# The last 34 rows of w_down: three small loads into 46 partitions, or seven, four of which bring two rows each into one partition

## The chip, the cores and the metric

The kernel runs on one core of one Trainium2 chip. The metric is the device time of one execution in microseconds (us). The kernel before takes 376.3 us, the median of 3 runs (376.07 to 376.39). PE is TensorE, DVE is VectorE, ACT is ScalarE, POOL is GpSimd, SP is SyncE, whose only work here is to issue DMAs.

## The reference, cut to what matters

One decode step for two batch rows, all float32: a layer norm, attention of 32 heads over the last 2048 keys and values of the cache, a bilinear GLU beside it, and the sum of both with x.

```python
xn = _layernorm(x)                                  # x: 2 x 1 x 512
q = xn @ wq                                         # 32 heads of 128
p = softmax(q . k_cache[:, :, -2048:] * 128**-0.5)
A = (p . v_cache[:, :, -2048:]) @ wo                # 4096 x 512
h = (xn @ w_gate) * (xn @ w_up)                     # 1376 wide
B = h @ w_down                                      # w_down: 1376 x 512
out = x + A + B
```

Nearly all bytes are keys, values and weights, each read once: some 159 MB.

## The kernel before, in words

**The stream.** The host lays keys, values and nearly all weights out in one array, `stream`, in the order of use. `blocks()` (lines 89 to 114) lists the loads, and `pump()` (182 to 203) issues them on SP's queue: first a small tile `first` (x and constants), then big `step` loads of up to 128 x 15872 floats (7936 KB) into three rotating buffers. A buffer is free when the last field in it has been used; `done()` (205 to 212) counts that, and calls `pump()`, which issues the next load into it. So the first three step loads are issued at the start, and the fourth waits for the buffer of the first (keys of heads 0 to 2), which DVE leaves after its third sum.

**The heads.** For each head DVE multiplies the keys by q (`products`) and sums along 128 elements (`sums`), 4.4 us each; POOL, ACT and DVE make the softmax; PE weighs the values and projects with `wo`, three heads behind.

**The GLU.** `project_gu` makes gate and up from the second step load, `gate()` (444 to 466) multiplies them and turns the 1376 values h into columns, with matmuls that each take a piece of h and an ACT copy out of PSUM each. `down`, `down_rest` (490 to 498) and `down_half` multiply by w_down. 1376 rows are 10 chunks of 128 and 96 more; of these 62 lie with x in the field `wr` of the stream.

**The tail.** The last 34 rows lie in an input of their own, `tail`, and come into the tile `wd_tail`, one row of 2 KB to a partition: 20 rows in partitions 0 to 19, 12 in 32 to 43, 2 in 44 and 45. `TG` and `TR` (46, 47) say so: runs of `OWN` = 4 rows, with an unused row in the input after each run, so that a load isn't one straight piece. Three loads on SP's queue (219 to 222) bring them, issued right behind the first three step loads. POOL clears the tile first (171). `gate()` makes the fitting columns of h in two pieces (462 to 466), and `down_rest` uses all 46 partitions in one product of two columns by 512 (497). `PADS` (49) are unused tiles that place the others in memory.

**Semaphores.** Each DMA signals its landing on one of eight semaphores, named DMAHW0 to DMAHW7, which the framework deals out in turn in the order of issue. A DMA that gets a semaphore that an earlier one had waits, on the issuing queue, until that earlier one has landed. All DMAs here but the first store are issued on SP, which works through its waits and issues strictly in order.

Of the kernel before, what the change touches and what calls it, by code (L numbers as in the profile page):

```python
# [8 lines left out]
F32 = mybir.dt.float32  # L9
# [7 lines left out]
P = 128  # L17
B, D, H, DH, SK, F = 2, 512, 32, 128, 8192, 1376
# [4 lines left out]
NFB = -(-F // FB)  # L23
# [5 lines left out]
M = B  # L29
# [12 lines left out]
RX = HP  # L42
FX = RX - M
FT = FR - FX
OWN = 4
TG = [(0, 5), (32, 3), (32 + 3 * OWN, 1)]
TR = [OWN, OWN, FT - 8 * OWN]
TP = TG[-1][0] + TR[-1]
PADS = 480, 376


def k(h):
# [36 lines left out]
def blocks():  # L89

    def wd(n):
        return [("wd", i, D) for i in range(*WD[n])]

    def gu(half):
        n = NC * (FH[half][1] - FH[half][0])
        return [("wg", half, n), ("wu", half, n)]

    ones = [("pick", 0, 8 * B), ("rows", 0, NFB * B)]
    first = [("x", 0, B * NC)] + ones + [("w", 0, NC * DH)]
    loads = [[("w", 1, CQ - NC * DH)] + k(0) + k(1) + k(2), gu(0) + k(3) + gu(1)]  # L100
    loads += [v(0) + wd(0) + [("wr", 0, HD)] + k(LAG + 1) + v(1)]
    order = [(h - (h >= EARLY), k, h) for h in range(LAG + 2, H - 1)]
    order += [(h + 0.5, v, h - LAG) for h in range(LAG + 2, H - 1)]
    order.sort(key=lambda n: n[0])
    loads += packed([f for _, fields, h in order for f in fields(h)])
    loads += [k(H - 1) + v(H - 1 - LAG) + wd(1)]
    out = [(("f", 0), first)] + [(("s", i), fields) for i, fields in enumerate(loads)]
    late, last = ("s", len(loads)), ("s", len(loads) + 1)
    out += [(late, v(H - 3) + [("vh", 0, CK // B)]), (late, v(H - 2)[:1])]
    out += [(last, [("vh", 1, CK // B)])]  # L110
    out += [(last, v(H - 2)[1:] + [("wo", H - 1, CO)] + wd(2))]
    halves = [("wh", (c, n), HD) for n in range(2) for c in range(WD[-1][1], NFC)]
    out += [(last, wd(3) + halves[:2])]
    return out + [(last, halves[i : i + 1]) for i in range(2, len(halves))]
# [33 lines left out]
def kernel(  # L148
# [8 lines left out]
    nc = tc.nc  # L157
    pe, dve, act, sp = (InOrder(tc, e) for e in (nc.tensor, nc.vector, nc.scalar, nc.sync))
# [3 lines left out]
    const = ctx.enter_context(tc.tile_pool(name="const", bufs=1))  # L162
# [4 lines left out]


    const.tile([P, PADS[0]], F32, name="pad0")
    wd_tail = const.tile([TP, D], F32, name="wd_tail")  # L170
    nc.gpsimd.memset(wd_tail, 0.0)

    todo, at = [], 0
    for key, fields in blocks():
# [30 lines left out]
    def done(kind, i):  # L205
        nonlocal held
        _, key = got.pop((kind, i))
        left[key] -= 1
        if left[key] == 0 and key[0] != "f":
            del tiles[key]  # L210
            held -= 1
            pump()
# [3 lines left out]
    pick = got["pick", 0][0].rearrange("p (r s b) -> p r s b", s=2, b=B)  # L216
    rows = got["rows", 0][0]

    g0 = 0
    for (r0, n), m in zip(TG, TR):  # L220
        sp.dma_start(wd_tail[r0 : r0 + n * m, :], tail[g0 : g0 + n, :m, :])
        g0 += n
    carry = rows[:M, :M]

    mean_w = const.tile([P, P], F32, name="mean_w")
# [6 lines left out]
    acc, acc_g = acc_t[:M, :], acc_t[:, :P]  # L232
# [15 lines left out]
    tr = ps_c.tile([P, 4 * P], F32, name="tr")  # L248
# [175 lines left out]

    hT = const.tile([P, 4, NFB, M], F32, name="hT")

    hX = const.tile([P, 3, M], F32, name="hX")
    dve.memset(hX, 0.0)

    def project_gu(half):  # L430
# [13 lines left out]
    def gate():  # L444
        g_sb = small.tile([P, FB], F32, name="o_sb", bufs=2)
        act.copy(g_sb, gu_ps[0])
        h_sb = small.tile([P, FB], F32, name="o_sb", bufs=2)
        dve.tensor_tensor(h_sb, g_sb, gu_ps[1], op=ALU.mult)
        for i in range(4):
            t = tr[:, P + i * P // 2 : P + i * P // 2 + NFB * B]  # L450
            pe.matmul(t, h_sb[:, i * P : (i + 1) * P], rows, start=True, stop=True)
            act.copy(hT[:, i, :, :], t.rearrange("p (n b) -> p n b", b=B))
        f = (NFC % 4) * P
        own = slice((NFB - 1) * B, NFB * B)
        for i in range(2):
            t = tr[HP * i : HP * i + RX, P + P // 4 : P + P // 4 + NFB * B]
            pe.matmul(t, h_sb[:, f - M : f + FX], rows, start=True, stop=True)
            act.copy(hX[HP * i : HP * i + RX, i, :], t[:, own])
            one = rows[HP * i : HP * i + M, 2 * i * B : 2 * i * B + B]
            act.copy(hX[HP * i : HP * i + M, i, :], one)  # L460
        f += FX
        for r0, r1 in ((0, TG[0][1] * OWN), (TG[1][0], TP)):
            t = tr[r0:r1, P + 3 * P // 4 : P + 3 * P // 4 + NFB * B]
            pe.matmul(t, h_sb[:, f : f + r1 - r0], rows, start=True, stop=True)
            act.copy(hX[r0:r1, 2, :], t[:, own])
            f += r1 - r0

    def down(n):
        for c in range(*WD[n]):
            if n < 2:  # L470
                pe.matmul(
                    acc, hT[:, c % 4, c // 4, :], got["wd", c][0],
                    start=False, stop=(c == WD[1][1] - 1),
                )
            else:
                accumulate(hT[:, c % 4, c // 4, :], got["wd", c][0])
            done("wd", c)
# [12 lines left out]
    def down_rest():  # L490
        wr = got["wr", 0][0]
        for i in range(2):
            pe.matmul(
                acc[:, HD * i : HD * i + HD], hX[: HP + RX, i, :], wr[: HP + RX],
                start=False, stop=False,
            )
        pe.matmul(acc, hX[:TP, 2, :], wd_tail, start=False, stop=False)
        done("wr", 0)


# [28 lines left out]
    for h in (H - 4, H - 3):  # L529
        products(h)  # L530
        if h == H - 3:
            for i, n in enumerate((FB, FB, FB, 448)):
                pe.matmul(
                    spare[:, :n], mean_w, got["k", h][0][:, i * FB : i * FB + n],
                    start=True, stop=True,
# [54 lines left out]
    down(3)  # L590
    const.tile([P, PADS[1]], F32, name="pad1")
    acc_late = spare[:, :HP]
# [18 lines left out]
def laid_out(x):  # L611

    import numpy as np

    a = x["A_x"].reshape(B, D)
    first = {
        kind: np.zeros((P, w), a.dtype) for kind, _, w in blocks()[0][1][:3]
    }
    first["x"][:] = a.reshape(B, P, NC).transpose(1, 0, 2).reshape(P, B * NC)
    for b in range(B):  # L620
        for r in range(4):
            for s in range(2):
                first["pick"][8 * s + 4 * b + r :: 32, (2 * r + s) * B + b] = 1.0
        for n in range(NFB):
            first["rows"][32 * n + b, n * B + b] = 1.0
    cache = {
        kind: x[name][:, :, SK - W :, :].reshape(B, H, P, J * DH).transpose(1, 2, 0, 3)
        for kind, name in (("k", "A_k_cache"), ("v", "A_v_cache"))
    }
    wq = x["A_wq"].reshape(P, NC, H // HG, GC).transpose(2, 0, 1, 3)  # L630
    wo = x["A_wo"].reshape(H, P, D)
    gu = {
        kind: x[name].reshape(P, NC, F)
        for kind, name in (("wg", "B_w_gate"), ("wu", "B_w_up"))
    }
    wd = x["B_w_down"]
    rest = wd[NFC * P :]
    mixed = np.zeros((2, HP, HD), a.dtype)
    mixed[:] = np.concatenate([a, rest[:FX]]).reshape(RX, 2, HD).swapaxes(0, 1)

    def field(kind, i):
        if kind in first:
            return first[kind]
        if kind == "k":
            return cache[kind][i].reshape(P, CK)
        if kind == "v":
            h, p0, p1 = i
            return cache[kind][h].reshape(P, CK)[:, p0 * FB : p1 * FB]
        if kind == "w":
            return (wq[0][:, :, DH:] if i else wq[0][:, :, :DH]).reshape(P, -1)  # L650
        if kind == "wq":
            return wq[i // HG + 1][:, i % HG, :]
        if kind == "wo":
            return wo[i]
        if kind == "wr":
            return mixed.reshape(P, HD)
        if kind == "vh":
            return cache["v"][H - 1][:, i]
        if kind == "wh":
            c, n = i  # L660
            return wd[c * P : (c + 1) * P].reshape(P, 4, 2, HP)[:, :, n].reshape(P, HD)
        if kind == "wd":
            return wd[i * P : (i + 1) * P]
        return gu[kind][:, :, FH[i][0] : FH[i][1]].reshape(P, -1)

    parts = [
        np.concatenate([field(kind, i) for kind, i, _ in fields], axis=1).ravel()
        for _, fields in blocks()
    ]
    groups_of = np.zeros((sum(n for _, n in TG), OWN + 1, D), a.dtype)  # L670
    r = FX
    for g in range(len(groups_of)):
        m = OWN if g < 8 else TR[-1]
        groups_of[g, :m] = rest[r : r + m]
        r += m
    return {
        "tail": groups_of,
        "stream": np.concatenate(parts),
    }

# [35 lines left out]
```

## Time and profile before

| | |
|---|---|
| time, median of 3 runs | 376.3 us |
| time of the profiled execution | 376.45 us |
| its span, first to last instruction | 374.7 us |
| read from HBM | 159.47 MB |
| mean of the DMA engines over the span | 426 GB/s |
| busy: PE, DVE, ACT, POOL | 69%, 79%, 15%, 7% |
| mean granted TensorE clock | 0.827 |

The span leaves out 1.75 us of the execution's time, before its first and after its last instruction. In the profile's rows the line is L132 for all that goes through the recording helper, so that rows are told apart by tiles: `out<-in`. A row of a timeline begins with start and duration in us, and ends with the engine's idle time ahead of it and what ended that. "DMA to landing" is from the start of the issuing instruction to the last of its data. A DMA share is the mean over 16 DMA engines; in windows of a few us it can go over 1, since a packet is counted where it begins.

### The profile page before, as it was taken

To read this page: it belongs to the slowest core of one execution; us is meant where nothing else is said; L and a number is where in the kernel's file an instruction comes from. 1 tells how busy PE (TensorE), PEld (TensorE's weight loads), DVE (VectorE), ACT (ScalarE), POOL (GpSimd) and SP (SyncE) were. 2 spreads that over 40 slices of the span, in tenths; PEclk is the share of its full clock that TensorE was granted. 3 is DMA by queue.
4 is the path that set the end of the run, shared out by engine and by line. 5 is a ranking of instruction groups with operands and counts; after the bars stand their busy time and mean duration, and the time that the engine had idled before them with its cause. 6 is when DMAs were issued, how large, how long until landed. Compare 5 with 4: busy or idle time off the path is not lost.

```text
span 374.7 us, 2900 instructions
## 1 busy us (share of the span) xinstructions
PE 259.6 (69%) x1108; PEld 89.9 (24%) x1108; DVE 294.7 (79%) x145; ACT 57.3 (15%) x260; POOL 25.7 (7%) x75
## 2 busy tenths in 40 slices
PE   3166696884597882685968705896565855599897
PEld 3132123231222221122312202222111211133244
DVE  3069999369979569999369999894599999999760
ACT  1002011110202210020112002112010210112131
POOL 1000000000001000000100000010000000000010
PEclk9999697799576886597788975889666899689999
DMA  8999999999999999999999999999999999999996
GB/s 344 420 438 467 466 408 441 434 434 428 429 428 434 434 434 434 429 434 434 434 429 428 434 434 434 434 429 435 434 434 434 435 427 434 434 434 420 422 419 266
DMA packets 4232, 159.70 MB, mean 426 GB/s; under 512 B 730, under 2 KB 986, under 8 KB 1276
## 3 DMA queue, kind: packets, MB, share of 16 engines
q1 hardware_dynamic: 4076, 159.50, 98.7%
q8 instruction: 8, 0.13, 0.1%
q10 hardware_dynamic: 144, 0.03, 0.0%
q14 instruction: 4, 0.03, 0.0%
HBM read 159.47 MB, written 0.07 MB: 426 GB/s over the span
## 4 chain that ended last, share of the span: by engine, by line
DMA 66%; PE 18%; DVE 14%; ACT 1%; issue 1%; SPq 0%; DVEq 0%
DMA step<-in_stream_dram 66%; DVE s L132 7%; DVE step L132 7%; PE q L132 6%; PE o_ps L132 6%; PE acc L132 4%; PE tr L132 2%; ACT o_sb L132 1%; ACT oT L132 0%; DVE m L132 0%; DVE o_out L132 0%; SPq L132 0%; DVE rec L132 0%; DVEq L132 0%
## 5 line engine op out<-in xcount | busy, mean ns | idle before, releaser
L132 DVE TENSOR_TENSOR step<-step,q 128x4096 f32<-128x4096 f32 x31 | 136.8, 4412 | 45.2 <-DMA step<-in_stream_dram 41.1
L132 DVE TENSOR_REDUCE s<-step 128x32 f32<-128x4096 f32 x32 | 141.4, 4419 | 1.1
L132 PE MATMUL o_ps<-step,p 128*16 128x512 f32 x512 | 76.1, 659 | 45.3 <-DMA step<-in_stream_dram 45.3
L132 PE MATMUL q<-step,xnb 128*128 128x512 f32 (+1 forms) x128 | 76.1, 742 | 31.9 <-DMA step<-in_stream_dram 31.9
L132 PEld LDWEIGHTS q<-step,xnb 128*128 128x128 f32 x128 | 29.2, 244 | 84.1 <-issue 67.1
L132 PE MATMUL acc<-step,oT 128*2 128x512 f32 (+1 forms) x88 | 39.6, 612 | 8.5 <-ACT oT L132 8.5
L132 PE MATMUL tr<-first,o_sb 128*128 128x2 f32 (+4 forms) x192 | 29.9, 274 | 15.8 <-ACT o_sb L132 11.9
L132 PEld LDWEIGHTS o_ps<-step,p 128*16 128x16 f32 x512 | 13.7, 100 | 98.0 <-DMA step<-in_stream_dram 54.7
L132 PEld LDWEIGHTS tr<-first,o_sb 128*128 128x128 f32 (+2 forms) x192 | 27.2, 216 | 39.8 <-ACT o_sb L132 33.7
L132 ACT COPY o_sb<-o_ps 128x512 f32<-128x512 f32 x23 | 13.5, 586 | 145.7 <-PE o_ps L132 145.6
L331 POOL PARTITION_ALL_REDUCE mm<-m x32 | 11.5, 358 | 240.2 <-DVE rec L132 135.4
L132 ACT ACTIVATE nm<-mm 128x2 f32<-128x2 f32 x32 | 6.6, 206 | 128.6 <-POOL mm L331 128.6
L347 POOL PARTITION_ALL_REDUCE sum<-rs x32 | 12.8, 400 | 97.7 <-ACT p L132 97.7
L132 ACT ACTIVATE p<-s,nm 128x16 f32<-128x16 f32 x64 | 19.2, 300 | 1.0
L132 PE MATMUL o_ps<-step,xn 128*2 128x512 f32 (+1 forms) x48 | 14.9, 683 | 5.9 <-DMA step<-in_stream_dram 5.9
L132 ACT ACTIVATE oT<-tr,rec 128x1 f32<-128x1 f32 x64 | 12.1, 260 | 27.9 <-PE tr L132 27.9
L132 DVE TENSOR_TENSOR step<-step,tr 128x4096 f32<-128x4096 f32 x1 | 4.4, 4422 | 15.2 <-DMA step<-in_stream_dram 15.2
L132 ACT ACTIVATION_READ_ACCUMULATOR p<-s,nm 128x1 f32 x64 | 12.0, 187 | 0.0
L132 PE MATMUL q<-xnb,mean_w 128*128 128x512 f32 (+5 forms) x26 | 10.2, 500 | 0.0
L132 PEld LDWEIGHTS acc<-step,oT 128*2 128x2 f32 x88 | 4.2, 87 | 21.6 <-ACT oT L132 12.1
L132 DVE RECIPROCAL rec<-sum 128x2 f32<-128x2 f32 x32 | 5.0, 155 | 4.1 <-POOL sum L347 4.1
L132 PEld LDWEIGHTS o_ps<-step,xn 128*2 128x2 f32 x48 | 2.9, 97 | 17.9 <-issue 11.1
(45 smaller groups left out, 48.9 us busy)
## 6 DMA issues: line engine op xcount, KB each, us to landing
step<-in_stream_dram SPq DMA_DIRECT2D x15, 7936.0 KB, 34.4
step<-in_stream_dram SPq DMA_DIRECT2D x1, 7808.0 KB, 38.7
step<-in_stream_dram SPq DMA_DIRECT2D x1, 7680.0 KB, 20.8
step<-in_stream_dram SPq DMA_DIRECT2D x1, 7552.0 KB, 57.4
step<-in_stream_dram SPq DMA_DIRECT2D x1, 4864.0 KB
step<-in_stream_dram SPq DMA_DIRECT2D x1, 3328.0 KB, 19.5
step<-in_stream_dram SPq DMA_DIRECT2D x1, 2048.0 KB, 23.9
step<-in_stream_dram SPq DMA_DIRECT2D x1, 1280.0 KB, 19.0
```

The costliest lines, as they stand in the source:

```text
L132: made = call(*args, **kwargs)
L331: nc.gpsimd.partition_all_reduce(mm, m, P, bass_isa.ReduceOp.max)
L347: nc.gpsimd.partition_all_reduce(sum_t[h], rs, P, bass_isa.ReduceOp.add)
```

## The change

The 34 rows get other places. 26 lie one to a partition: 12 in partitions 32 to 43 (runs of 4), 10 in 4 to 13 and 4 in 14 to 17 (runs of 2). The other 8 lie in pairs, in partitions 0 to 3: `wd_tail` gets a second slot of 512 floats, and each of these partitions gets both its slots by a load of its own, one straight piece of 4 KB. That makes seven loads of the tail for three. `gate()` makes three pieces of h for two, `hX` gets a fourth plane, and `down_rest` makes two products, one over 44 partitions and one over the 4 partitions of the second slot. The padding is changed such that the step buffers stay where they were; the tiles between `wd_tail` and them move by 160 bytes.

```diff
-TG = [(0, 5), (32, 3), (32 + 3 * OWN, 1)]
-TR = [OWN, OWN, FT - 8 * OWN]
-PADS = 480, 376
+OWN, SLOTS = 4, 2
+TG = [(32, 3, OWN), (OWN, 5, 2), (OWN + 5 * 2, 2, 2)]
+TA = FT - 4 * OWN
+TP = 32 + 3 * OWN
+PADS = 8, 336
...
-    wd_tail = const.tile([TP, D], F32, name="wd_tail")
-    nc.gpsimd.memset(wd_tail, 0.0)
+    wd_tail = const.tile([TP, SLOTS, D], F32, name="wd_tail")
+    nc.gpsimd.memset(wd_tail[:, 0, :], 0.0)
...
-    for (r0, n), m in zip(TG, TR):
-        sp.dma_start(wd_tail[r0 : r0 + n * m, :], tail[g0 : g0 + n, :m, :])
-        g0 += n
+    for r0, n, m in TG:
+        src = tail[at : at + n * (m + 1), :].rearrange("(g m) d -> g m d", g=n)
+        sp.dma_start(wd_tail[r0 : r0 + n * m, 0, :], src[:, :m, :])
+        at += n * (m + 1)
+    for p in range(OWN):
+        src = tail[at + SLOTS * p : at + SLOTS * (p + 1), :]
+        sp.dma_start(wd_tail[p : p + 1], src.rearrange("(p s) d -> p s d", p=1))
...
-    hX = const.tile([P, 3, M], F32, name="hX")
+    hX = const.tile([P, 2 + SLOTS, M], F32, name="hX")
...
-        for r0, r1 in ((0, TG[0][1] * OWN), (TG[1][0], TP)):
+        for r0, r1, i in ((0, TA, 0), (32, TP, 0), (0, OWN, 1)):
...
-        pe.matmul(acc, hX[:TP, 2, :], wd_tail, start=False, stop=False)
+        for i, k in enumerate((TP, OWN)):
+            pe.matmul(acc, hX[:k, 2 + i, :], wd_tail[:k, i, :], start=False, stop=False)
```

SP's queue at the start of the program, before: the small tile, three step loads (128 x 15360, 15616 and 15104 floats), the tail, and the fourth and fifth step load, with the semaphores for which each waits.

```order
L132 DMA first<-in_stream_dram 128x542
L132 DMA step<-in_stream_dram 128x15360
L132 DMA step<-in_stream_dram 128x15616
L132 DMA step<-in_stream_dram 128x15104
L132 DMA wd_tail<-in_tail_dram 20x1x512 [waits Pool_49]
L132 DMA wd_tail<-in_tail_dram 12x1x512
L132 DMA wd_tail<-in_tail_dram 2x512
L132 DMA step<-in_stream_dram 128x15872 [waits DMAHW1_49,DVE_49,PE_49]
L132 DMA step<-in_stream_dram 128x15872 [waits DMAHW0_49,DMAHW2_49,DVE_49,PE_49]
```

The same stretch after.

```order
L132 DMA step<-in_stream_dram 128x15104
L132 DMA wd_tail<-in_tail_dram 12x1x512 [waits Pool_49]
L132 DMA wd_tail<-in_tail_dram 10x1x512
L132 DMA wd_tail<-in_tail_dram 4x1x512
L132 DMA wd_tail<-in_tail_dram 1x1024
L132 DMA wd_tail<-in_tail_dram 1x1024 [waits DMAHW0_49]
L132 DMA wd_tail<-in_tail_dram 1x1024 [waits DMAHW1_49]
L132 DMA wd_tail<-in_tail_dram 1x1024 [waits DMAHW2_49]
L132 DMA step<-in_stream_dram 128x15872 [waits DMAHW3_49,DVE_49,PE_49]
L132 DMA step<-in_stream_dram 128x15872 [waits DMAHW4_49,DVE_49,PE_49]
```

Dealt out in turn, DMAHW0 is the small tile's, DMAHW1 to 3 the first three step loads', and the tail's begin with DMAHW4. Before, the fourth step load is the eighth DMA and gets DMAHW7, which none had; the DMAHW1 for which it waits is the landing of the first step load, whose buffer it takes. After, it is the twelfth DMA and gets DMAHW3, which the third step load had, so it waits for that one's landing; the three last pieces of the tail ahead of it wait for the small tile and for the first and second step load.

PE where `gate()` ends and `down_rest` stands, before and after as a difference (`o_sb` is h there, `tr` the PSUM tile of the columns): first the end of `gate()`.

```order
 L132 MATMUL tr<-first,o_sb 128x6 x4
 L132 MATMUL tr<-first,o_sb 64x6 x2
-L132 MATMUL tr<-first,o_sb 20x6
-L132 MATMUL tr<-first,o_sb 14x6
+L132 MATMUL tr<-first,o_sb 18x6
+L132 MATMUL tr<-first,o_sb 12x6
+L132 MATMUL tr<-first,o_sb 4x6
```

One matmul more stands there, and ACT has one copy more behind it, from `tr` to `hX`. Then PE's rows of `down_rest`, which sums into `acc`:

```order
 L132 MATMUL acc<-step,hT 2x512 x2
 L132 MATMUL acc<-step,hX 2x256 x2
-L132 MATMUL acc<-wd_tail,hX 2x512
+L132 MATMUL acc<-wd_tail,hX 2x512 x2
 L132 MATMUL q<-step,xnb 128x512 x2
```

Here too one matmul more stands, ahead of the projections of q for the next heads.

More of the change, by code (lines that the diff above doesn't have):

```diff
@@ L44 @@
 FT = FR - FX
-OWN = 4
-TG = [(0, 5), (32, 3), (32 + 3 * OWN, 1)]
-TR = [OWN, OWN, FT - 8 * OWN]
-TP = TG[-1][0] + TR[-1]
-PADS = 480, 376
+OWN, SLOTS = 4, 2
[3 more added lines that the diff above has]
+PADS = 8, 336
 def k(h):
@@ L217 @@
     rows = got["rows", 0][0]
-    g0 = 0
-    for (r0, n), m in zip(TG, TR):
-        sp.dma_start(wd_tail[r0 : r0 + n * m, :], tail[g0 : g0 + n, :m, :])
-        g0 += n
+    at = 0
+    for r0, n, m in TG:
[5 more added lines that the diff above has]
+        sp.dma_start(wd_tail[p : p + 1], src.rearrange("(p s) d -> p s d", p=1))
     carry = rows[:M, :M]
@@ L461, in gate @@
         f += FX
-        for r0, r1 in ((0, TG[0][1] * OWN), (TG[1][0], TP)):
-            t = tr[r0:r1, P + 3 * P // 4 : P + 3 * P // 4 + NFB * B]
+        for r0, r1, i in ((0, TA, 0), (32, TP, 0), (0, OWN, 1)):
+            at = P + 3 * P // 4 + 8 * i
+            t = tr[r0:r1, at : at + NFB * B]
             pe.matmul(t, h_sb[:, f : f + r1 - r0], rows, start=True, stop=True)
-            act.copy(hX[r0:r1, 2, :], t[:, own])
+            act.copy(hX[r0:r1, 2 + i, :], t[:, own])
             f += r1 - r0
@@ L669, in laid_out @@
     ]
[L670 to L675, printed above, removed]
+    tail = []
+    for r0, n, m in TG:
+        r = FX + (r0 if r0 < 32 else r0 - 32 + TA)
+        spaced = np.zeros((n, m + 1, D), a.dtype)
+        spaced[:, :m] = rest[r : r + n * m].reshape(n, m, D)
+        tail.append(spaced.reshape(-1, D))
+    slots = [rest[r : r + OWN] for r in (FX, len(rest) - OWN)]
+    tail.append(np.stack(slots, axis=1).reshape(-1, D))
     return {
-        "tail": groups_of,
+        "tail": np.concatenate(tail),
         "stream": np.concatenate(parts),
```

## Prediction

> **What bounds the kernel now.** I read the page first, for its DMA rows, its queues and the chain that ended last.
>
> ```profile
> span 374.7 us, 2900 instructions
> DMA  8999999999999999999999999999999999999996
> q1 hardware_dynamic: 4076, 159.50, 98.7%
> q8 instruction: 8, 0.13, 0.1%
> DMA 66%; PE 18%; DVE 14%; ACT 1%; issue 1%; SPq 0%; DVEq 0%
> step<-in_stream_dram SPq DMA_DIRECT2D x15, 7936.0 KB, 34.4
> ```
>
> The 16 DMA engines are busy at 90% or more in every slice but the first and the last, and 98.7% of their time over the span goes to queue 1, the stream. The chain gives 66% to DMA; its DVE and PE pieces are no refutation, since it follows a load back to the instruction that let it be issued, even where the load then stood in line. The last row shows the line: a 7936 KB load lands 34.4 us after its issue. How long its data alone take, the table by windows tells (the last two columns are the DMA share and GB/s).
>
> ```profile
> 95.00:340.00 245.00, 168.97 (x614) 54.13 (x618) 209.22 (x93) 37.00 (x176) 17.40 (x46) 0.77 1.00 434
> 370.00:371.00 1.00, 1.00 (x20) 0.97 (x23) 0.00 (x0) 0.17 (x2) 0.00 (x0) 1.00 0.83 328
> 371.00:372.00 1.00, 1.00 (x46) 0.71 (x40) 0.00 (x0) 0.55 (x4) 0.00 (x0) 1.00 0.49 171
> ```
>
> From 95 to 340 us the engines have a share of 1.00 and 434 GB/s: 7936 KB (8.13 MB) take 18.7 us. So a load stands in line for 34.4 - 18.7 = 15.7 us: loads are issued long before the engines need them, and no engine of the compute side sets the pace. The last two rows show that the 16 engines don't end together: the share falls over some 2 us, and the last engine's last piece is what PE's last products need. A stall of the stream that hits all engines goes to the end of the span in full. So I looked for the places where the change could let the stream run dry. There are three kinds of change: what SP does at the start, what the 34 rows take on the engines, and what PE and ACT do more.
>
> **SP's queue and the fourth step load.** The start of the program, by SP's timeline, and the landings of what is issued in the first 4 us, with the DMA row of those 4 us (40 slices of 0.1 us):
>
> ```profile
> 0.72 0.39 SPq L132 DMA_DIRECT2D first<-in_stream_dram  x1
> 1.16 1.36 SPq L132 DMA_DIRECT2D step<-in_stream_dram  x3
> 2.09 0.43 SPq L132 DMA_DIRECT2D step<-in_stream_dram  x1
> 2.57 2.22 SPq L132 DMA_DIRECT2D wd_tail<-in_tail_dram  x3
> 49.05 0.36 SPq L132 DMA_DIRECT2D step<-in_stream_dram  x1
> ```
>
> ```profile
> DMA  0000000000000000099980639999999000000000
> step<-in_stream_dram SPq DMA_DIRECT2D x1, 7808.0 KB, 38.7
> step<-in_stream_dram SPq DMA_DIRECT2D x1, 7680.0 KB, 20.8
> step<-in_stream_dram SPq DMA_DIRECT2D x1, 7552.0 KB, 57.4
> ```
>
> Load 1 (7680 KB) is issued at 1.16 and lands at 22.0, load 2 (7808 KB, issued between the two, at about 1.6) at 40.3, load 3 (7552 KB, issued at 2.09) at 2.09 + 57.4 = 59.5. Load 4 is issued at 49.05, which is when DVE leaves the buffer of load 1:
>
> ```profile
> 44.55 4.43 DVE s L132
> 59.56 4.42 DVE L132 TENSOR_TENSOR step<-step,q 128x4096 f32<-128x4096 f32 x1 [0.76 <-DMA step<-in_stream_dram]
> 78.25 4.42 DVE L132 TENSOR_TENSOR step<-step,q 128x4096 f32<-128x4096 f32 x1 [7.51 <-DMA step<-in_stream_dram]
> ```
>
> The sum of the third head ends at 44.55 + 4.43 = 48.98, load 4 goes out 0.07 us later, some 9 us before the engines have done load 3. The second row confirms load 3's landing: DVE waits until 59.56 for it. In the changed program load 4 carries another wait: four more DMAs stand ahead of it, it gets the semaphore of load 3, and waits for load 3's landing. Queued behind it on SP are load 5 and all others. The waits of the three last tail pieces, on the small tile, load 1 and load 2, are over by 40.3 and delay nothing.
>
> So load 4 is issued at 59.53 + 0.07 = 59.6 instead of 49.05. By then the engines have nothing of the stream left. From issue to the first data the DMA row above shows 1.0 us (issue at 0.72, first busy slice 1.7). The stores at the end, again onto idle engines, show a little less (40 slices of 0.0475 us from 372.8):
>
> ```profile
> 372.85 0.37 ACTq L132 DMA_DIRECT2D out_dram<-o_out  x1
> 373.17 0.35 SPq L132 DMA_DIRECT2D out_dram<-o_out  x1
> DMA  0000000000000000000169841069851000000000
> out_dram<-o_out SPq DMA_DIRECT2D x1, 32.0 KB, 1.5
> ```
>
> The slices that begin to fill are at 373.70 and 374.04, 0.85 and 0.87 us after the issues. I take 0.9: data flow again at 60.5.
>
> The Trainium skill, "DMA: Bandwidth & Descriptors", Specifications, gives about 0.6 us to the first byte for a DMA from SP's queue; by it the data would flow at 60.2 and the sum below be smaller by 0.3. The same page, "Why a DMA increments its semaphore by 16 and not by 1", says to give every DMA in flight a semaphore of its own, since two in flight on one can't be told apart; this rule speaks against the change, because eleven loads at the start over eight semaphores can only be kept apart by such waits. In the trace of before the seven loads at the start share none and none of them stands still for another, which agrees with it.
>
> When do the engines run dry? From load 2's landing, 7552 KB at 434 GB/s take 17.8 us: 40.3 + 17.8 = 58.1. A landing comes about 0.4 us after the last data (the store of 373.17 lands at 374.67, its slices end near 374.25), so 57.7. That load 3's last part lands only at 59.5 has another reason:
>
> ```profile
> q8 instruction: 1, 0.02, 0.1%
> ```
>
> In the first 60 us (and again in the window 48 to 60) one packet of queue 8, an instruction fetch of 16 KB, takes one engine of the sixteen, which ends load 3 some 1.4 us after the rest. Load 4's new wait needs all sixteen. So 15 engines stand still from 57.7 to 60.5, **2.8 us**, the held one for 1.4. The page counts eight such fetches, seven of them later: they hold other engines in both kernels, so at the end the last engine is one held later, and carries the 2.8, not the 1.4.
>
> Should the fetch come at another time, load 3 lands at 58.1, load 4 goes out at 58.2, data flow at 59.1, and 1.4 us are lost.
>
> **The 34 rows on the engines.** They stand behind load 3 on SP's queue, before and after, and so are moved when load 3 is done. A DMA engine moves 434/16 = 27.1 GB/s, 2 KB in 76 ns. The trace doesn't show how many engines take them: spread over 16 they take 34 x 76/16 = 0.16 us, all on one 2.6 us. Before, this delays load 4 on the busiest engine; after, it lies in the standstill, and is recovered on the engine that has it, unless that is not the last engine at the end. Between nothing and the 2.6 us I take 0.4, since three loads in runs of four rows use several engines (the busiest would have 34/16 to some ten rows, 0.16 to 0.76 us). The four rows of 4 KB take 4 x 151 ns even if all lie on one engine, 0.6 us in a hole of 2.8: nothing. If one such row were cut into 4-byte pieces (the stores' 144 packets take 7.9% of 16 engines in 1.9 us, 17 ns each), 4096 pieces would take 4.4 us over 16 engines, 1.6 beyond the hole.
>
> **PE and ACT.** One product more of the gate's and one of `wd_tail`:
>
> ```profile
> 62.90 0.24 PE L132 MATMUL tr<-first,o_sb 128*20 128x6 f32 x2 [0.24 <-ACT hX L132]
> 63.37 0.22 PE L132 MATMUL tr<-first,o_sb 128*14 128x6 f32 x2 [0.24 <-ACT hX L132]
> 74.51 1.02 PE L132 MATMUL acc<-wd_tail,hX 46*2 46x512 f32 x2
> 75.46 1.98 PE L132 MATMUL q<-step,xnb 128*128 128x512 f32 x4
> 82.59 35.30 SPq L132 DMA_DIRECT2D step<-in_stream_dram  x3
> 58.10 38.84 DMA step<-in_stream_dram
> ```
>
> From piece to piece of the gate 0.47 us pass, with ACT's copy in between; the product of `wd_tail` takes 0.95 until the next begins: 1.4 us on PE. They delay what follows on PE up to the issue of load 6 at 82.59. The engines then have loads 4 and 5 until 96.9 (58.10 + 38.84), so 14 us cover 1.4. Cost 0; without the cover it would be 1.4. DVE has 7.51 us of waiting ahead of 78.25, so nothing of it arrives there. The tail's data, moved in the standstill, are there by 74.51. The extra 160 bytes in the addresses of small tiles, the wider memset and POOL's clear of 44 rows instead of 46 (done before 3 us) cost nothing: the stream's buffers stay where they are.
>
> **Sum.** 2.8 - 0.4 = **+2.4 us**. The profiled execution of 376.45 would be 378.85; the median lies 0.15 below it, so **378.7 us**.
>
> **The rivals.** (a) The fetch falls outside the first 58 us: 1.4 - 0.4 = +1.0, **377.3**. The fetch is tied to how far an engine's program has come, and the programs are alike up to the gate at 58 us; chance 0.1. (b) The standstill is real, but something else sets the end and takes it up: no change, **376.3**. For it speaks that PE is fully busy from 370 to 372; against it that it waits for the stream again and again, that its last products take the last loads, and the share of 1.00. Chance 0.05. (c) Faster: the wait for load 3 costs nothing, because load 3 has landed before DVE leaves the buffer of load 1. Then only the balance of the rows counts, up to 0.7 us on the busiest engine: **375.6**. It decides at one point, whether the landing precedes 48.98; in the profile it comes at 59.5, 10.5 us too late, and two loads of 18 us can't be gone by then. Chance 0.03, mostly for a semaphore that counts otherwise than I read it. (d) The 4 KB rows are cut small: another +1.6, **380.3**. Odd shapes cost the issuer something (2.22 us on SP for the three tail loads, 1.36 for three step loads), but a row of 4 KB is one straight piece on both sides. Chance 0.03. That the change doesn't spread the rows better is possible, and without effect on the time, as they lie in the hole.
>
> **How the numbers follow.** My case has 0.79. Its own bounds: restart 0.85 to 1.2 us (the slowest engine may begin 0.2 after the first), recovery 0.8 to 0, so +1.9 to +3.1. With (a) the range is 377.3 to 379.5. A measurement of this kernel can tell 0.2%, 0.75 us, from no change. Slower: my case, (a) and (d), 0.92, less a little for a small shift that ends within 0.75: 0.91. Same: (b) and that little, 0.06. Faster: (c), 0.03.
>
> **What would show it.** Right: SP's timeline has the fourth step load issued near 59.6 and the fifth right behind it, not at 49 and 58; a window of 0.1 us slices has all engines idle for about a us just before 60.5; DVE's wait at 78.25 ends near 79.6 instead; load 5 lands near 98.5 to 99.3 instead of 96.9; from there to the end all is later by 2 to 3 us, at 434 GB/s. The tail's packets lie between 57.7 and 59. Wrong: load 4 at 49 still, or a shift at 78 us that is gone at 340 (then something else sets the pace), or a shift that appears elsewhere, such as a second gap in the DMA row.

## The result and the profile after

| | before | after |
|---|---|---|
| time, median | 376.2 us (5 runs, 375.98 to 376.39) | 380.3 us (5 runs, 380.22 to 380.51) |
| ratio | | 1.011, 95% interval 1.0096 to 1.0125 |
| span of the profiled execution | 374.7 us | 378.6 us |

The change makes the kernel 4.1 us slower. The forecast was slower by 2.4, with a range up to 379.5: the right way and, as the experiments show, the right mechanism, but one term of its sum was too small, and the time lies outside the range.

The page of the changed kernel, where it answers to the rows shown before:

```profile
span 378.6 us, 2916 instructions
DMA  8999996999999999999999999999999999999996
GB/s 341 435 474 449 415 404 255 449 456 423 444 430 436 436 429 431 429 429 429 429 429 431 430 429 436 429 438 430 436 456 436 424 443 436 429 436 406 413 422 256
DMA packets 4232, 159.70 MB, mean 422 GB/s; under 512 B 734, under 2 KB 990, under 8 KB 1276
q1 hardware_dynamic: 4076, 159.50, 97.9%
DMA 62%; DVE 19%; PE 16%; ACT 1%; issue 1%; SPq 0%; DVEq 0%
```

The same bytes, but the seventh slice (56.8 to 66.3 us) has a 6 where before there was a 9, and 255 GB/s. It is the only such slice. The chain's shares moved by a few per cent (DMA from 66% to 62%, DVE from 14% to 19%, PE from 18% to 16%), which says nothing here: the chain follows one path, and the hole lies across all of them.

SP's timeline from 20 to 62 us, and DVE's rows that wait for the stream:

```profile
22.09 18.64 SPq L132 DMA_DIRECT2D wd_tail<-in_tail_dram  x2
59.72 0.83 SPq L132 DMA_DIRECT2D step<-in_stream_dram  x2
59.65 4.42 DVE L132 TENSOR_TENSOR step<-step,q 128x4096 f32<-128x4096 f32 x1 [0.72 <-DMA step<-in_stream_dram]
81.28 4.42 DVE L132 TENSOR_TENSOR step<-step,q 128x4096 f32<-128x4096 f32 x1 [8.88 <-DMA step<-in_stream_dram]
101.32 4.42 DVE L132 TENSOR_TENSOR step<-step,q 128x4096 f32<-128x4096 f32 x1 [1.81 <-DMA step<-in_stream_dram]
```

The last two pieces of the tail go out when load 1 and load 2 have landed (22.1 and 40.5), load 4 at 59.72, 0.07 after the DVE row that shows load 3 landed, instead of at 49.05. Load 4 lands by 81.28 (before: 78.25) and load 5 by 101.3 (before: 58.10 + 38.84 = 96.9). That is 3.0 and 4.4 later, on both sides of the 3.9 of the span. A landing goes by the last of 16 engines: before, the one that a fetch had held ended load 4 last; after, a packet of queue 8 lies in load 5's time (81 to 101 us), where before none did (78 to 97).

The hole itself, in slices of 0.2 us from 57 to 65, which the text counts from 0. Each row of digits and GB/s counts a packet in the slice in which it begins; a row of 62 KB to a partition is one packet, so that 16 engines at work show a wave of beginnings every 2.34 us. First the kernel before:

```profile
DMA  0799999000700799997000700799990007000999
GB/s 0 317 676 2028 420 1024 645 0 0 0 317 0 0 317 952 1587 635 952 317 0 0 0 317 0 0 317 1905 635 635 1270 0 0 0 317 0 0 0 952 1270 952
```

Then the changed one, with the windows on both sides of the hole (span of the window, five engines' busy time, clock, DMA share, GB/s):

```profile
DMA  0001121100000000009909900000000007999700
GB/s 0 0 31 41 62 92 51 51 20 0 0 0 0 0 0 0 0 0 2222 1905 0 317 635 0 0 0 0 0 0 0 0 0 0 317 1587 1587 1270 317 0 0
```

```profile
59.00:60.00 1.00, 0.75 (x4) 0.61 (x4) 0.35 (x1) 0.16 (x1) 0.31 (x1) 0.69 0.00 0
60.00:60.60 0.60, 0.35 (x3) 0.29 (x2) 0.60 (x1) 0.16 (x1) 0.00 (x0) 0.50 0.00 0
64.00:78.00 14.00, 12.64 (x38) 3.53 (x38) 4.84 (x4) 2.04 (x10) 0.73 (x2) 0.56 1.00 435
95.00:340.00 245.00, 161.46 (x603) 52.17 (x604) 208.42 (x93) 37.08 (x176) 17.31 (x46) 0.77 1.00 432
```

Before, the waves come at slices 1 to 6, 13 to 18 and 25 to 30, 12 slices apart, each with one late beginning behind it (slices 10, 22 and 34), that of the engine that the fetch held. After, only the small rows of the tail begin in the first wave's place (slices 2 to 8), no row begins from 58.8 to 60.6, the first wave of load 4 comes at slices 18 to 22, **and the next at 33 to 37, 15 slices later, not 12**.

The queue's row gives the size of that: its share counts the whole time of each packet that begins in the window. Here are the 16 rows that begin from 60.6 to 61.6, and the next 16, from 63.7 to 64.6:

```profile
q1 hardware_dynamic: 16, 1.02, 316.8%
q1 hardware_dynamic: 16, 1.02, 260.7%
```

The first rows took 3.168 x 1.0 = 3.17 us each in the mean, the next 2.607 x 0.9 = 2.35: the first rows after the hole took 0.8 us longer than others do. From 64 on the rate is that of before, 435 and 432 GB/s (before: 435 and 434), and nothing is made up.

### The profile page after: what moved, and what is told of

Read it like the earlier page. It is cut to its first block, busy times and chain, and to the rows that moved or that the text cites. A ratio compares the mean times of both kernels' runs of the same rounds, so it can differ in the third digit from the quotient of the medians.

```text
span 378.6 us, 2916 instructions
## 1 busy us (share of the span) xinstructions
PE 261.4 (69%) x1112; PEld 91.4 (24%) x1112; DVE 294.7 (78%) x145; ACT 57.5 (15%) x261; POOL 25.6 (7%) x75
## 4 chain that ended last, share of the span: by engine, by line
DMA 62%; DVE 19%; PE 16%; ACT 1%; issue 1%; SPq 0%; DVEq 0%
DMA step<-in_stream_dram 62%; DVE step L132 9%; DVE s L132 9%; PE o_ps L132 5%; PE acc L132 5%; PE q L132 3%; PE tr L132 3%; ACT o_sb L132 1%; ACT oT L132 0%; DVE m L132 0%; DVE o_sb L132 0%; DVE o_out L132 0%; SPq L132 0%; DVE rec L132 0%; ACT hT L132 0%
## 5 line engine op out<-in xcount | busy, mean ns | idle before, releaser
L132 PE MATMUL o_ps<-step,p 128*16 128x512 f32 x512 | 75.3, 650 | 45.1 <-DMA step<-in_stream_dram 45.1
L132 PE MATMUL q<-step,xnb 128*128 128x512 f32 (+1 forms) x128 | 74.7, 731 | 33.1 <-DMA step<-in_stream_dram 33.1
L132 PE MATMUL acc<-step,oT 128*2 128x512 f32 (+1 forms) x88 | 41.7, 638 | 8.6 <-ACT oT L132 8.6
L132 PE MATMUL tr<-first,o_sb 128*128 128x2 f32 (+5 forms) x194 | 31.6, 281 | 16.3 <-ACT o_sb L132 11.8
L132 PEld LDWEIGHTS tr<-first,o_sb 128*128 128x128 f32 (+3 forms) x194 | 28.9, 226 | 40.8 <-ACT o_sb L132 34.0
```

The costliest lines, as they stand in the source:

```text
L132: made = call(*args, **kwargs)
```

## The experiments

Three theories were set against each other. A: all of it is load 4's wait for load 3's landing. B: small loads cost about 1 us each, and there are four more. C: the new layout costs it, with its products, columns, rows of 4 KB and addresses.

**The four rows of 4 KB in one load** (`one_load`):

```diff
-    for p in range(OWN):
-        src = tail[at + SLOTS * p : at + SLOTS * (p + 1), :]
-        sp.dma_start(wd_tail[p : p + 1], src.rearrange("(p s) d -> p s d", p=1))
+    for p, n in ((0, 4),):
+        src = tail[at + SLOTS * p : at + SLOTS * (p + n), :]
+        sp.dma_start(wd_tail[p : p + n], src.rearrange("(p s) d -> p s d", p=n))
```

> The changed kernel, with its four rows of 4 KB brought by one load of 4 partitions instead of four loads: places in memory, products, columns and addresses are those of the change, but the fourth step load is now the ninth DMA and shares its semaphore with the small first tile, landed at 3 us. Theory A (all of the change's 4.1 us is the fourth step load's wait for the third's landing): 376.2 +- 0.5, fourth load issued near 49. Theory B (every small load costs about 1 us by itself, four more of them 4 us): one more than before, 377.2. Theory C (the new layout: products, columns, 4 KB rows, addresses): 380.3 still.

Measured: 376.4 us, ratio to before 1.0004 (0.9995 to 1.0013). Everything of the change is in it but the number of loads, and all of the 4.1 us is gone. C falls, and B too. SP's rows:

```profile
49.27 9.40 SPq L132 DMA_DIRECT2D step<-in_stream_dram  x2
83.98 0.33 SPq L132 DMA_DIRECT2D step<-in_stream_dram  x1
```

Load 4 is back at 49.3. Load 6 goes out at 83.98 instead of 82.59: that is the 1.4 us of the added matmuls on PE, and the loads that stand in the engines' queue hide it, as the times show.

**Two of the four rows in one load** (`six_loads`), the same lines with `((0, 1), (1, 1), (2, 2))`:

> The changed kernel with two of its four rows of 4 KB in one load: six loads of the tail for seven, so that the fourth step load shares the second step load's semaphore, landed at 40.3, before its buffer is free at 49.0. Theory A: the wait is met in time, 376.2 +- 0.5 (a threshold between six and seven loads). Theory B: three more small loads than before, 379.2. Theory C: 380.3.

Measured: 376.28 us, 1.0006 (0.9997 to 1.0016). Six loads cost nothing, seven cost 4.1: a threshold, where B had a slope.

```profile
49.00 10.93 SPq L132 DMA_DIRECT2D step<-in_stream_dram  x2
```

Load 4 goes out at 49.00. Here it is load 5 that got load 3's semaphore: from the start of the first issue to the end of the second 10.9 us pass, not 9.4, since load 5 waits for load 3's landing at 59.5. That wait costs nothing, because load 4 is in the engines' queue by then. It isn't the wait that has a price, but the queue that it lets run dry.

**The kernel before, with its load of 20 rows cut into five** (`before_seven`):

```diff
-    for (r0, n), m in zip(TG, TR):
-        sp.dma_start(wd_tail[r0 : r0 + n * m, :], tail[g0 : g0 + n, :m, :])
-        g0 += n
+    for i, ((r0, n), m) in enumerate(zip(TG, TR)):
+        for g in range(n) if i == 0 else (0,):
+            g1, r1 = (1, r0 + g * m) if i == 0 else (n, r0)
+            sp.dma_start(wd_tail[r1 : r1 + g1 * m, :], tail[g0 : g0 + g1, :m, :])
+            g0 += g1
```

> The kernel before, with its load of 20 rows cut into five of 4 rows each to the same partitions: nothing else of the change, but seven loads of the tail, so that the fourth step load waits for the third's landing. Theory A: 380.3 +- 0.5, fourth load issued near 59.7, engines idle for about 3 us. Theory B: 380.2, with the fourth load issued near 49. Theory C: 376.2.

Measured: 380.23 us, 1.011 (1.0096 to 1.0124), the same as the change, without any of its layout. B had this time too, but with load 4 issued near 49; it goes out at 59.83.

```profile
59.83 0.83 SPq L132 DMA_DIRECT2D step<-in_stream_dram  x2
81.47 4.42 DVE L132 TENSOR_TENSOR step<-step,q 128x4096 f32<-128x4096 f32 x1 [9.47 <-DMA step<-in_stream_dram]
```

With these three, A is shown from both sides. The rest asks for the size.

**A cover of known length.** With six tail loads, load 3 is cut in two in `blocks()`. That deals load 3's first part the semaphore that load 4 gets, so that load 4 waits for the first part while the second is still to be moved. The cut at 3.0 us (`split_3us`), the others alike:

```diff
+    vs, wo1 = v(1)
+    third = loads[2][:-2] + [("v", (1, 0, 4), 4 * FB)]
+    out[3:4] = [(("s", 2), third), (("s", 2), [("v", (1, 4, 8), 4 * FB), wo1])]
```

> Six loads of the tail as in the run with six, and the third step load cut in two, of 12544 and 2560 floats to a partition (the second 1.31 MB, 3.0 us of the stream), so that the fourth step load waits for the first part's landing while the second part is still to be moved. Theory A with a standstill that the cover shortens by its own length: the first part lands near 56.6, data of the fourth load flow near 57.8, the engines are dry from 57.6 on: 0.2 to 1.0 us lost, 376.5 to 377.2. A rival on the size (a fixed cost for load 4 to restart, whatever is queued ahead of it): 379 to 380.

> As the run with the third step load cut at 3.0 us, but with a second part of 512 floats to a partition, 0.26 MB, 0.6 us of the stream. Theory A with a standstill that cover shortens by its own length: 4.1 - 0.6 = 3.5 us over before, 379.7 (379.3 to 380.1). Rival on the size (any load that waits for all of the load ahead costs the same, whatever covers it): 380.3.

> As the run with the third step load cut at 3.0 us (which lost 1.8 us), but with a second part of 4608 floats to a partition, 2.36 MB, 5.4 us of the stream. Theory A: the first part lands near 53.9, the fourth load is issued near 54, its data could flow at 55, the engines are busy until 57.6: nothing is lost, 376.2 to 376.6. If the 1.8 us of the run with 3.0 us came from the cut itself (one DMA more, other order of semaphores) and not from too short a cover, it stays near 378.

> The third step load cut with a second part of 1536 floats to a partition, 0.79 MB, 1.8 us of the stream. The cover of 0.6 us left 3.6, that of 3.0 left 1.8, that of 5.4 left 0.1. If each us of cover is worth about 0.75 us: 2.7 over before, 378.9. If cover is worth its own length and the run with 3.0 us stood apart for another reason (its data reach the engines unevenly): 2.3, 378.5.

> As the last, with a second part of 3584 floats to a partition, 1.84 MB, 4.2 us. At 0.75 us a us of cover: 0.9 over before, 377.1. If the price falls to nothing as soon as new data arrive before the old ones end (issue at about 55.1, data at 56.1 against 57.6): 376.3.

The change itself was run once more in the set of the last two (`change_again`):

> The change itself once more, beside the three others of this set on one chip. 380.3 +- 0.3.

| cover, us of stream | median, us | ratio to before (95%) | above before, us |
|---|---|---|---|
| 0 (`change_again`) | 380.16 | 1.0107 (1.0093 to 1.0121) | 4.0 |
| 0.6 | 379.73 | 1.0102 (1.0087 to 1.0117) | 3.6 |
| 1.8 | 378.21 | 1.0062 (1.0050 to 1.0075) | 2.1 |
| 3.0 | 377.95 | 1.0049 (1.0037 to 1.0062) | 1.8 |
| 4.2 | 376.48 | 1.0015 (1.0006 to 1.0024) | 0.3 |
| 5.4 | 376.22 | 1.0005 (0.9996 to 1.0014) | 0.1 |

Two of the five expectations failed: the cover of 3.0 us left 1.8 where 0.2 to 1.0 was expected, and that of 1.8 did better than both of its values (378.9 at 0.75 a us, 378.5 at its own length). A fixed price for any such wait, whatever covers it, is out: 4.0 falls to 0.3. The whole table is near a straight line of (4.0 - 0.3)/4.2 = 0.9 us for each us of cover, off it by up to half a us. The intervals of 0 and 0.6 overlap, and so do those of 1.8 and 3.0; whether 3.0 stands apart from its neighbours by more than noise stays open. SP's rows for the covers of 3.0, 4.2 and 5.4 us, one kernel each:

```profile
56.30 3.37 SPq L135 DMA_DIRECT2D step<-in_stream_dram  x2
```

```profile
55.11 4.70 SPq L135 DMA_DIRECT2D step<-in_stream_dram  x2
```

```profile
54.04 5.82 SPq L133 DMA_DIRECT2D step<-in_stream_dram  x2
```

Before, the engines begin load 4 from 57.2 on, about half of them by 57.8 (the waves above); I count from 57.6. Issued at 54.04, 3.6 us ahead of that, load 4 costs nothing, also with the wait kept and the cut made, so the cut itself is free; issued at 55.11, 2.5 ahead, it costs 0.3; at 56.30, 1.3 ahead and with its first data due at 57.3 by the 1.0 us of the program's first load, still 1.8. Here a load that comes just in time by its first byte comes too late.

**A lead of small rows** (`lead`, `lead_again`). The changed kernel with load 4 cut behind 512 floats:

```diff
+    head = next(f for f in loads[3] if f[0] in ("wq", "wo"))
+    rest = [f for f in loads[3] if f is not head]
+    out[4:5] = [(("s", 3), [head]), (("s", 3), rest)]
```

> The changed kernel with its fourth step load cut in two: a lead of 512 floats to a partition (0.26 MB, rows of 2 KB), then the other 15360. The wait for the third load is kept. What it asks is why the restart cost more than the 0.9 us I took: if the first rows of 62 KB are slow to get going on an idle engine, rows of 2 KB get going faster and 0.5 to 0.8 us of the 4.1 come back, 379.5 to 379.8; if any first row costs that much, or the engines fill at the pace at which the load is handed out, 380.2 to 380.5.

> The run with a lead of 2 KB rows ahead of the fourth step load once more, now beside the change on one chip, since its 3.8 us over before could not be told from the change's 4.1. If big first rows are a part of the restart's price: 0.3 to 0.5 below the change (its fourth load landed 0.4 us earlier). If not: no difference.

Measured: 379.91 us, 1.0104 (1.0090 to 1.0117), and again 379.97, 1.0106 (1.0090 to 1.0121), beside 380.16 for the change on the same chip: not to be told apart. In the trace load 4's rest lands 0.4 us earlier than in the change:

```profile
59.79 1.30 SPq L135 DMA_DIRECT2D step<-in_stream_dram  x3
80.87 4.42 DVE L135 TENSOR_TENSOR step<-step,q 128x4096 f32<-128x4096 f32 x1 [9.70 <-DMA step<-in_stream_dram]
```

The profiled spans are 0.4 shorter too, 378.2 and 378.1 against 378.6 and 378.5, but the medians differ by 0.2, and their intervals overlap. The size of the first rows is at most a small part of the price; why the first rows are slow isn't settled.

**The 34 rows in two straight loads** (`even`), from the kernel before, in partitions 0 to 33 of the tile:

```diff
-TG = [(0, 5), (32, 3), (32 + 3 * OWN, 1)]
+TG = [(0, 32), (32, FT - 32)]
...
+    for r0, n in TG:
+        sp.dma_start(wd_tail[r0 : r0 + n, :], tail[r0 : r0 + n, :])
```

> The kernel before with the 34 rows in partitions 0 to 33, brought by two loads, of 32 rows and of 2, each from one straight piece: no run breaks, so that the 32 rows may spread over more engines, and no new wait. If the busiest engine's share of the tail (0.4 us in my sum) counts at the end: 375.5 to 376.0. If it doesn't, because the last engine at the end is one that an instruction fetch held: 376.2 +- 0.2.

Measured: 376.29 us, 1.0014 (0.9994 to 1.0034). No gain. In none of the four versions that were run without the hole (before, `one_load`, `six_loads` and `even`) is the way in which the tail's rows are spread worth anything at the end. No version beat the kernel before.

## Why the prediction fell short, point by point

- **The mechanism: right.** Load 4 waits for load 3, is issued at 59.72 (forecast 59.6) with load 5 right behind it, all engines stand still ahead of 60.6 (forecast 60.5), and the shift goes to the end: 374.7 to 378.6 in span.
- **"2.8 us" of standstill: too small, and the step that failed.** It was made of a last byte at 57.7 and first data at 60.5, as if all engines began together and the stream were at full speed from its first byte. The waves show two things in its place. The middle of the first wave moved from about 57.7 to between 60.8 and 60.9, some 3.1 us: the engines don't all begin 0.9 us after the issue, but 0.9 to 1.9 after it. And their first rows take 3.17 us instead of 2.35, a term that the sum put at nothing. 3.1 + 0.8 = 3.9, which is the 3.9 us of the spans. The lead's small rows didn't take this price away, so it belongs to the restart and not to the 62 KB rows alone. My upper bound for the restart, 1.2 us, allowed 0.2 us between the first engine and the slowest, where about 0.9 passed, and nothing for slow first rows: that is why the range ended at 379.5. Two signs were missed by it too: DVE's wait ended at 81.3, not 79.6, and load 5 landed at 101.3, not 98.5 to 99.3, with a fetch in it besides.
- **"0.4 recovered" from the tail: too much, and not seen at the end.** The tail's rows do lie in the hole (slices 2 to 8), and before they lay ahead of load 4's rows. By the prediction's own rate they are 34 x 76/16 = 0.16 us an engine in the mean, and the 3.1 us above, taken from beginning to beginning of load 4's rows, hold that already: there is nothing more to subtract. `even`, which spreads them otherwise, gains nothing, so the busiest engine's share, from which the 0.4 was taken, isn't seen in the time.
- **The engine held by the fetch: right that it doesn't count.** Load 4's landing, which that engine set before, moved by 3.0 us; the end moved by 3.9, the price of the 15 others.
- **PE and ACT at nothing: right,** and shown: load 6 goes out 1.4 us later in `one_load`, at no cost. Addresses, clear and memset at nothing: right, by the same run.
- **Rival (d)** named 380.3, the measured time, for another reason. It didn't happen: were the 4 KB rows cut into small pieces, the packets under 512 B would have grown by thousands; they grew from 730 to 734, and the number of all packets stayed 4232. `before_seven` has the time without such rows.
- **The first-byte figure of the Trainium skill,** "DMA: Bandwidth & Descriptors", Specifications, about 0.6 us, would have made the sum smaller still. The trace shows 0.9 to 1.1 from issue (59.72) to the first row (in the slice from 60.6 to 60.8), and the whole price here was 4.1 us.
- **The Trainium skill's rule of one semaphore for each DMA in flight** (the same page, "Why a DMA increments its semaphore by 16 and not by 1") is about telling DMAs apart, and no run here shows two mixed up. What the runs show is the price of the waits that keep them apart: nothing as long as the earlier DMA lands while another load still stands in the queue (`six_loads`), and 4.1 us where it was the last big one in the queue.

## What to carry to other kernels

Count the DMAs that are issued before the stream is under way, and look in the built order for the semaphore that each later load shares: one small load more can turn a free wait into one that drains the queue. Ask how far ahead of the dry queue a load of the stream is issued; its first-byte time alone wasn't enough here: 3.6 us ahead cost nothing, 2.5 ahead 0.3, 1.3 ahead 1.8, and not at all ahead about 4. When you price such a gap, measure it from the rows before to the rows after it, and ask how long the first rows after it take: here 3.1 us were the gap with its late beginnings, and 0.8 were slow first rows.

## What was not expected of the hardware

After some 3 us without a row of the stream the 16 engines begin within about 1 us of each other, and their first rows take 3.17 us in the mean where 2.35 is usual (the two rows of queue 1 above). The time that this costs is never made up: from 95 to 340 us the stream moves 434 GB/s before and 432 after.

The trace of before has a smaller case of it, which could have been read ahead of the forecast. From 2.7 to 3.1 us, where load 1 begins, queue 1's packets take 690.0% of 0.4 us, 2.76 us an engine; without the last rows of the small tile this leaves some 2.6 us for load 1's first rows, an estimate, and the next take 2.28 (415.2% of 0.55 us, from 5.2 on). That both have one cause isn't shown.
